# Transforming by mirrored pairs of places: the spectral mixing kernel with 64-point stages in quarters of the array

## The chip, the cores and the metric

The kernel runs on one core of one Trainium2 chip. The metric is the device time of one launch in microseconds; for the kernel before, the median of three runs is given. Where a profile is read, it is one profiled execution, which has a time and a span of its own.

## What is computed

The input x has 8 batches of 3008 places and 256 channels. Each batch is filtered in the frequency domain along the places, and every row then goes through a two-layer network with a "snake" activation:

```python
X = np.fft.rfft(x, axis=1)
y = np.fft.irfft(X * (filt_r + 1j * filt_i), n=3008, axis=1)     # (8, 3008, 256)
h = y.reshape(24064, 256) @ w_in                                # (24064, 2048)
s = np.sin(alpha * h)
out = (h + s * s / (alpha + 1e-9)) @ w_out                      # (24064, 256), float32
```

## The kernel before

3008 is 47 x 64, and a transform runs as a 47-point stage and a 64-point stage, in fp16 with fp32 sums. A place is `R*m + r` with m from 0 to 46 and r from 0 to 63. Only 24 of the 47 frequencies s of the first stage are kept, since x is real.

For a batch b after the first the steps are:

- `load_x`: the batch goes to SBUF through the POOL queue, cast from fp32 to fp16, with two parts of its rows on partitions 0 to 46 and 64 to 110.
- `f1`: the 47-point stage, four calls of eight matmuls. Each uses 47 rows and 48 columns of one quarter (64 x 64) of the array, streams 512 columns, and has the same table `wq`. Four PSUM banks are emptied by ACT and DVE into `asb`, and `asb` is written to a DRAM scratch `scr1`.
- `shuffle1`: reads the scratch back as `bint`, with the places r and the two complex parts on the 128 partitions and the frequency s on the free axis. It is three DMAs on SP's queue.
- `f2x`: the 64-point stage, 24 matmuls of 128 x 128 by 256 columns. Each s has a table of its own in `wb`, since the twiddle factors are inside.
- `swap` and `product`: the product with the filter. Real and imaginary parts lie 64 partitions apart, so from the third batch on two DMAs from SBUF to SBUF swap the halves; the first and second batch have other ways.
- `f2g`, `shuffle2`, `f3`: the way back, again with 24 matmuls with tables of their own (`wg`), a DRAM scratch `scr2`, and a 47-point stage by `we`, which gives the rows of the network transposed, in `yt`.

The network works in 47 chunks g of 512 rows. A chunk has 16 blocks j of the hidden layer: `mlp_in` (two matmuls of 512 columns into a bank `ph`, and on ACT the sine into `vt`), `square` on DVE, and one chunk later the second layer, `mlp_out` for chunks 0 to 3 and `fast_out` (seven products in place of eight, with sums on DVE in `fast_sum`) for the later ones but the last. `out_last` does the last chunk alone, and `store_out` writes 128 rows at a time with DMAs on SP's queue, in the last chunk on SP's and ACT's.

The order is written by hand. A chunk is eight slots of two half slots; a half slot is one `mlp_in` and a share of the second layer. `plan` maps a half slot to the transform steps that are put in it, and `at(slot, f, ...)` fills it. While the network of one batch runs, the transform of the next is done between its matmuls. Every engine runs its instructions in program order.

The first batch can't hide behind a network. It stays on the chip: `f1_chip`, `turn1`, `f2x`, `product`, `g_chip`, `turn2` in an order of its own, with `keep_busy` matmuls of zeros between them. `fold_filter` copies the filter to the upper 64 partitions, and `negate_filter` changes its sign later.

PSUM has three banks `psf` (tag f) for the transform, three banks `psh` (tag ph) for `mlp_in`, and two `pso` for the second layer. `xt` and `bint` share one buffer (tag xb), and so do `asb` and `gsb` (tag ag).

`store_out` cuts a piece of n rows, where n is over 16, to a multiple of 16 and does the rest in a DMA of its own:

```python
n = min(GT - col, 128 - p)
n = n // 16 * 16 or n
```

Of the kernel before, what the change touches and what calls it, by code (L numbers as in the profile page):

```python
# [9 lines left out]
FP16 = mybir.dt.float16  # L10
FP32 = mybir.dt.float32
# [5 lines left out]
GT = 2 * MT  # L17


def dft_tables():  # L20

    m = np.arange(MT)
    k1 = np.arange(NK)
    ang = 2 * np.pi * np.outer(m, k1) / MT
    fa = np.concatenate([np.cos(ang), -np.sin(ang)], 1) / np.sqrt(MT)
    wa = np.zeros((MT, 2, 2, 2 * NK))
    wa[:, 0, 0] = fa  # L30
    wa[:, 1, 1] = fa
    wa = wa.reshape(2 * MT, 4 * NK)
    wa2 = wa.reshape(2 * MT, 4, NK).transpose(0, 2, 1).reshape(2 * MT, 4 * NK)

    we = wa.T.copy()
    we2 = wa2.T.copy()
    wq = np.zeros((2, 64, 64))
    wq[:, 0:MT, 0:2 * NK] = fa
    wq = wq.reshape(128, 64)
    r = np.arange(R)  # L40
    wb = np.zeros((2, R, NK, 128))
    wg = np.zeros((128, NK, 2, R))
    q = 1 / np.sqrt(R)
    d, j, di, ji = slice(0, 32), slice(32, 64), slice(64, 96), slice(96, 128)
    for s in range(NK):
        kd = s + MT * np.arange(32)
        kj = MT * np.arange(1, 33) - s
        td = 2 * np.pi * (np.outer(r, kd) % S) / S
        tj = 2 * np.pi * (np.outer(r, kj) % S) / S
        cd, sd, cj, sj = np.cos(td) * q, np.sin(td) * q, np.cos(tj) * q, np.sin(tj) * q  # L50
        wb[0, :, s, d], wb[1, :, s, d], wb[0, :, s, di], wb[1, :, s, di] = (
            cd, sd, -sd, cd)
        wb[0, :, s, j], wb[1, :, s, j], wb[0, :, s, ji], wb[1, :, s, ji] = (
            cj, -sj, -sj, -cj)
        wd = np.where((kd == 0) | (kd == S // 2), 1.0, 2.0)[:, None]
        wj = np.where(kj == S // 2, 1.0, 0.0 if s == 0 else 2.0)[:, None]
        wg[d, s, 0], wg[di, s, 0], wg[d, s, 1], wg[di, s, 1] = (
            wd * v.T for v in (cd, -sd, sd, cd))
        wg[j, s, 0], wg[ji, s, 0], wg[j, s, 1], wg[ji, s, 1] = (
            wj * v.T for v in (cj, -sj, -sj, -cj))  # L60

    wb = wb.reshape(2, 2, RP, NK * 128).transpose(2, 1, 0, 3).reshape(128, NK * 128)
    wg = wg.reshape(128, NK, 2, 2, RP).transpose(0, 1, 4, 3, 2).reshape(128, NK * 128)
    wgs = np.concatenate([wg[64:], -wg[:64]], 0)
    return [a.astype(np.float16) for a in (wq, wb, wg, we, wa2, we2, wgs)]

@with_exitstack
def kernel(
# [17 lines left out]
    wq_np, wb_np, wg_np, we_np, wa2_np, we2_np, wgs_np = dft_tables()  # L86
    wq_d = nc.inline_tensor(wq_np, name="wq_tbl")
    wb_d = nc.inline_tensor(wb_np, name="wb_tbl")
    wg_d = nc.inline_tensor(wg_np, name="wg_tbl")
    we_d = nc.inline_tensor(we_np, name="we_tbl")  # L90
    wa2_d = nc.inline_tensor(wa2_np, name="wa2_tbl")
    we2_d = nc.inline_tensor(we2_np, name="we2_tbl")
    wgs_d = nc.inline_tensor(wgs_np, name="wgs_tbl")
# [18 lines left out]
    wq = cpool.tile([128, 64], FP16, name="wq")  # L112
    we = cpool.tile([4 * NK, GT], FP16, name="we")
    wa2 = cpool.tile([GT, 4 * NK], FP16, name="wa2")
    we2 = cpool.tile([4 * NK, GT], FP16, name="we2")
    wb = cpool.tile([128, NK * 128], FP16, name="wb")
    wg = cpool.tile([128, NK * 128], FP16, name="wg")
    fri = cpool.tile([128, 2, NK, C], FP16, name="fri")
    w_in16 = tpool.tile([128, 2, DFF], FP16, name="w_in16", tag="tb")
    w_ina = cpool.tile([128, 2, DFF], FP16, name="w_ina")  # L120
# [6 lines left out]
    xt, asb, scr1, bint, xs, z, t2, gsb, scr2, gin, yt, vt, po, ot, x_dma, w_in_dma, filter_dma, swap_dma = (  # L127
# [7 lines left out]
    def load_x(b, parts=2):  # L135

        xt[b] = (xbpool if b else vpool).tile([128 if b else GT, RP, C], FP16, name="xt", tag="xb" if b else "vt")
        n = RP // parts
        for h in range(parts):
            for p0, p1, row, step in (((0, 32, 0, R), (32, MT, 32 * R, R), (64, 96, RP, R), (96, 64 + MT, 32 * R + RP, R))  # L140
                                      if b else ((0, 80, 0, RP), (80, GT, 80 * RP, RP))):
                x_dma[b, h] = nc.gpsimd.dma_start(  # L142
                    out=xt[b][p0:p1, n * h:n * h + n, :],
                    in_=dram(x, (b * S + row + n * h) * C, [[step * C, p1 - p0], [1, n * C]]))
                if b > 2 and h == p0 == 0:
                    gate(x_dma[b, 0], swap_dma[b - 1, 5])

    def f1(b, u):

        if u == 0:  # L150
            asb[b] = agpool.tile([128, 2, RP // 2, C], FP16, name="asb", tag="ag")
            scr1[b] = dpool.tile([RP, 4 * NK, C], FP16, name="scr1", tag="scr1")
        v, w2 = divmod(u, 2)
        ps = [(psh if i == 3 else psf).tile([128, 2, C], FP32, name="psa", tag="ph" if i == 3 else "f")
              for i in range(4)]
        for i in range(2):
            w = 2 * w2 + i
            for h in range(2):
                r0 = 16 * v + 8 * h + 2 * w
                for a in range(2):  # L160
                    nc.tensor.matmul(out=ps[2 * i + a][64 * h:64 * h + 64], lhsT=wq[64 * a:64 * a + MT],  # L161
                                     rhs=xt[b][64 * a:64 * a + MT, r0:r0 + 2, :], start=True, stop=True)
            for a in range(2):
                k = 8 * v + 2 * w
                (nc.vector.tensor_copy if a == 1 and not i else nc.scalar.copy)(  # L165
                    out=asb[b][0:112, a, k:k + 2, :], in_=ps[2 * i + a][0:112])
        if w2:
            for h in range(2):
                r0 = 16 * v + 8 * h
                for a in range(2):  # L170
                    nc.sync.dma_start(
                        out=scr1[b][r0:r0 + 8, 2 * NK * a:2 * NK * a + 2 * NK].rearrange("r q c -> q r c"),
                        in_=asb[b][64 * h:64 * h + 2 * NK, a, 8 * v:8 * v + 8, :])

    def f1_chip(k):

        for half in range(2):
            ps = (psf if half else psh).tile([128, 4, 4 * NK], FP32, name="psa0", tag="f" if half else "ph")
            for i in range(4):
                nc.tensor.matmul(out=ps[:, i, :], lhsT=xt[0][:, 4 * k + i, 128 * half:128 * half + 128],  # L180
                                 rhs=wa2, start=True, stop=True)
            (nc.vector.tensor_copy if half else nc.scalar.copy)(
                out=a_c[:, half, :, 16 * k:16 * k + 16].rearrange("p s (r a) -> p s r a", a=4),
                in_=ps.rearrange("p r (s a) -> p s r a", a=4))

    def turn1(t):

        ps = psh.tile([128, 2, C], FP32, name="pst1", tag="ph")
        for i in range(2):
            for half in range(2):  # L190
                nc.tensor.matmul(out=ps[:, i, 128 * half:128 * half + 128],
                                 lhsT=a_c[:, half, 2 * t + i, :], rhs=ident, start=True, stop=True)
        (nc.vector.tensor_copy if t in (0, 5) else nc.scalar.copy)(
            out=bint[0][:, 2 * t:2 * t + 2, :], in_=ps)

    def g_chip(k, half, i0=0, n=4, act=True):

        ps = (psh if half else pso).tile([128, 4, 128], FP32, name="psg0", tag="ph" if half else f"po{k % 2}")
        for i in range(i0, i0 + n):
            for v, w in ((z, wg), (t2, wgs)):  # L200
                nc.tensor.matmul(out=ps[:, i - i0, :], lhsT=v[k][:, i, 128 * half:128 * half + 128],
                                 rhs=w[:, 128 * (4 * k + i):128 * (4 * k + i) + 128],
                                 start=(v is z), stop=(v is t2))
        (nc.scalar.copy if act and (k, half) != (4, 1) else nc.vector.tensor_copy)(
            out=b_c[:, half, :, 4 * k + i0:4 * k + i0 + n, :],
            in_=ps[:, 0:n].rearrange("p s (r a) -> p r s a", a=4))

    def turn2(j):

        ps = (psf if j < 4 else pso).tile([4 * NK, 2, C], FP32, name="pst2", tag="f" if j < 4 else f"po{j % 2}")  # L210
        rows = b_c.rearrange("p h r s a -> p h r (s a)")
        for i in range(2):
            for half in range(2):
                nc.tensor.matmul(out=ps[:, i, 128 * half:128 * half + 128],
                                 lhsT=rows[:, half, 2 * j + i], rhs=ident, start=True, stop=True)
        (nc.scalar.copy if j in (0, 2, 3, 7, 8) else nc.vector.tensor_copy)(
            out=gin[0][:, 2 * j:2 * j + 2, :], in_=ps)

    def shuffle1(b):
        bint[b] = xbpool.tile([128, NK, C], FP16, name="bint", tag="xb")  # L220
        rows = scr1[b].rearrange("r (a s) c -> (r a) s c", s=NK)
        for sg in range(3):
            nc.sync.dma_start(out=bint[b][:, 8 * sg:8 * sg + 8, :],
                              in_=rows[:, 8 * sg:8 * sg + 8, :])

    def f2x(b, t):
        ps = psf.tile([128, 2, C], FP32, name="psx", tag="f")
# [493 lines left out]
```

## Time and profile before

| what | value |
|---|---|
| median of three runs | 790.77 us (790.77 to 792.18) |
| the profiled execution | 789.34 us |
| its span, first to last instruction | 787.5 us |
| granted TensorE clock, mean | 0.999 |
| PE busy | 773.4 us, 8623 matmuls |
| DVE busy | 696.1 us |
| ACT busy | 659.0 us |
| DMA | 74463 packets, 101.08 MB |
| end of the first stage (first `mlp_in`) | 35.2 us |
| last matmul | starts at 783.4 us |

Busy times are sums over the whole span; a matmul's duration includes its way through the array, so that durations overlap and the start-to-start time says what a matmul costs. A line number such as L161 is the line of the kernel before. "a<-b" reads "a is written from b". In a group, the numbers behind the first bar are busy time and mean duration, and behind the second the engine's idle time ahead of the group with what ended it.

### The profile page before, as it was taken

The page shows a single profiled execution, that of the slowest core. Times are in us where ns is not written, and L with a number is a line of the kernel's source. Part 1 is how long each engine was busy: PE and PEld are TensorE (multiplying, and loading weights), DVE is VectorE, ACT ScalarE, POOL GpSimd, SP SyncE. Part 2 cuts the span into 40 slices and gives each one's busy share as a digit, 9 for nine tenths or more (in the row PEclk, how much of TensorE's full clock was granted, in tenths as well). Part 3 has the DMA queues.
Part 4 walks back from the last instruction along what each step waited for, and adds up shares of the span by engine and source line. Part 5 has one row for each costly group of instructions (what it writes and reads, how often), then busy time and mean ns, then how long its engine had stood idle before and what let it go on. Part 6 is the DMA issues. An engine that isn't in the chain of part 4 may idle for free.

```text
span 787.5 us, 20811 instructions
## 1 busy us (share of the span) xinstructions
PE 773.4 (98%) x8623; PEld 561.5 (71%) x8623; DVE 696.1 (88%) x992; ACT 659.0 (84%) x1316; POOL 53.2 (7%) x104
## 2 busy tenths in 40 slices
PE   6899999999999999999999999999999999999998
PEld 4657666777677776777767777777767777777776
DVE  4896987899889998899898998899988999888894
ACT  4897988898888989798888888889888898777773
POOL 6600020002000020000200010000200000000000
PEclk9999999999999999999999999999999999999999
DMA  9977377434862367633865249623675234321122
GB/s 200 196 117 253 109 187 164 136 105 117 195 177 82 114 147 158 179 87 90 179 142 161 82 102 198 185 80 94 149 196 165 81 108 107 71 55 28 29 55 54
DMA packets 74463, 101.08 MB, mean 128 GB/s; under 512 B 7897, under 2 KB 54761, under 8 KB 72857
## 3 DMA queue, kind: packets, MB, share of 16 engines
q1 hardware_dynamic: 65136, 78.39, 36.8%
q0 software_dynamic: 8704, 21.24, 14.0%
q8 instruction: 67, 1.10, 0.6%
q14 instruction: 28, 0.22, 0.1%
q10 hardware_dynamic: 528, 0.13, 0.1%
HBM read 59.62 MB, written 46.66 MB: 135 GB/s over the span
## 4 chain that ended last, share of the span: by engine, by line
PE 91%; DMA 5%; DVE 2%; ACT 1%; issue 1%; POOL 0%; ACTq 0%; DVEq 0%; POOLq 0%
PE ph L312 40%; PE pf L399 37%; PE po L331 4%; PE psy L296 3%; PE psg L268 2%; PE psx L229 2%; PE psa L161 2%; DMA xt<-in_x_dram 1%; DMA bint<-scr 1%; DMA wgs<-wgs_tbl 1%; PE pe L438 1%; DMA w_in<-in_moe_w_in_dram 1%; ACT vt L314 1%; DMA wb<-wb_tbl 1%; PE psm L503 0%
## 5 line engine op out<-in xcount | busy, mean ns | idle before, releaser
L314 ACT ACTIVATE vt<-ph 128x512 f16<-128x512 f32 x688 | 408.2, 606 | 85.9 <-PE ph L312 76.2
L312 PE MATMUL ph<-yt,w_ina 128*128 128x512 f16 x1376 | 409.9, 380 | 0.0
L399 PEld LDWEIGHTS <-vt 128*128 128x128 f16 x3360 | 231.4, 98 | 104.7 <-DVE ot L413 0.9
L319 DVE TENSOR_TENSOR vt<-vt 128x2048 f16<-128x2048 f16 x188 | 229.3, 1220 | 19.1 <-ACT vt L314 17.8
L399 PE MATMUL pf<-w_out,vt 128*128 128x128 f16 x2016 | 174.5, 220 | 0.2 <-DVE ot L413 0.2
L399 PEld LDWEIGHTS <-s 128*128 128x128 f16 x1344 | 92.6, 98 | 39.8
L413 DVE TENSOR_TENSOR ot<-pf,ot 128x512 f32<-128x512 f32 (+1 forms) x168 | 93.4, 556 | 29.0 <-PE pf L399 26.1
L399 PE MATMUL pf<-tb,s 128*128 128x128 f16 x1344 | 116.2, 220 | 0.0
L399 PE MATMUL pf<-tb,vt 128*128 128x128 f16 x1344 | 116.2, 220 | 0.0
L312 PEld LDWEIGHTS <-w_ina 128*128 128x128 f16 x1376 | 107.0, 98 | 12.1 <-issue 9.6
L142 POOL DMA_DIRECT2D xt<-in_x_dram x72 | 36.6, 516 | 459.2 <-PE ph L312 354.0
L233 ACT CAST xs<-psx 128x512 f16<-128x512 f32 x94 | 56.1, 602 | 3.5 <-PE psx L229 1.1
L270 ACT CAST gsb<-psg 128x512 f16<-128x512 f32 x84 | 48.9, 590 | 4.3 <-PE psg L268 1.2
L358 DVE TENSOR_TENSOR vt<-vt 128x2048 f16<-128x2048 f16 x42 | 51.2, 1219 | 0.0
L358 DVE TENSOR_TENSOR s<-vt 128x2048 f16<-128x2048 f16 x42 | 51.2, 1219 | 0.0
L358 DVE TENSOR_TENSOR s<-s,vt 128x2048 f16<-128x2048 f16 x42 | 51.2, 1219 | 0.0
L358 DVE TENSOR_TENSOR vt<-vt,s 128x2048 f16<-128x2048 f16 x42 | 51.1, 1216 | 0.0
L314 ACT ACTIVATE vt<-ph,alpha_t 128x512 f16<-128x512 f32 x64 | 42.8, 711 | 6.0 <-PE ph L312 5.7
L165 ACT CAST asb<-psa 112x512 f16<-112x512 f32 x84 | 43.7, 596 | 4.6 <-PE psa L161 4.2
L298 ACT CAST yt<-psy 128x376 f16<-128x376 f32 (+45 forms) x126 | 46.4, 369 | 1.1 <-PE psy L296 0.2
L296 PE MATMUL psy<-we,gin 96*128 96x94 f16 x512 | 42.3, 205 | 0.3 <-ACT asb L165 0.3
L331 PE MATMUL po<-w_out,vt 128*128 128x256 f16 x256 | 37.1, 273 | 0.9 <-DVE ot L449 0.9
(96 smaller groups left out, 775.1 us busy)
## 6 DMA issues: line engine op xcount, KB each, us to landing
scr<-asb SPq DMA_DIRECT2D x56, 192.0 KB
bint<-scr SPq DMA_DIRECT2D x21, 512.0 KB
scr<-gsb SPq DMA_DIRECT2D x21, 512.0 KB
out_dram<-ot SPq DMA_DIRECT2D x31, 320.0 KB
t<-xs SPq DMA_DIRECT2D x72, 128.0 KB
xt<-in_x_dram POOLq DMA_DIRECT2D x24, 256.0 KB, 6.6
gin<-scr SPq DMA_DIRECT2D x7, 768.0 KB
out_dram<-ot SPq DMA_DIRECT2D x16, 256.0 KB
```

Source lines behind the costliest of these rows:

```text
L165: (nc.vector.tensor_copy if a == 1 and not i else nc.scalar.copy)(out=asb[b][0:112, a, k:k + 2, :], in_=ps[2 * i + a][0:112])
L233: (nc.vector.tensor_copy if b == 0 and t in (4, 5) else nc.scalar.copy)(out=xs[b, t // 2][:, t % 2 * 2:t % 2 * 2 + 2, :], in_=ps)
L270: nc.scalar.copy(out=gsb[b][:, 2 * t:2 * t + 2, :], in_=ps)
L296: nc.tensor.matmul(out=ps[:, t, :], lhsT=gin[b][:, 4 * a + t, 128 * cb:128 * cb + 128], rhs=we if b else we2, start=True, stop=True)
L298: (nc.vector.tensor_copy if G < 2 and cb == 0 else nc.scalar.copy)(out=yt[g][:, cb, :, lo:lo + n], in_=ps[:, :, 0:n])
L312: nc.tensor.matmul(out=ph, lhsT=(w_in16 if g < 4 else w_ina)[:, cb, 128 * jb:128 * jb + 128], rhs=yt[g][:, cb], start=(cb == 0), stop=(cb ...
L314: nc.scalar.activation(out=vt[g][:, jb, :], in_=ph, func=AFT.Sin, scale=alpha_t[:, jb:jb + 1] if g < 4 else 1.0)
L319: nc.vector.tensor_tensor(out=v4, in0=v4, in1=v4, op=ALU.mult)
L331: nc.tensor.matmul(out=po[g, h][:, i, :], lhsT=vt[g][:, k, ts] if k < 16 else yt[g][:, k - 16, t], rhs=w_out2[:, row(k), :], start=(n == 0 ...
L358: nc.vector.tensor_tensor(out=o, in0=a, in1=b, op=op)
L399: nc.tensor.matmul(out=ps[:, part, i], lhsT=a, rhs=b, start=first, stop=last)
L413: add = lambda out, in0, in1: nc.vector.tensor_tensor(out=out, in0=in0, in1=in1, op=ALU.add)
```

## The change

A place is now written as one of a mirrored pair: `R*m + (j + 0.5)` or `R*m - (j + 0.5)` about a shifted origin, for j from 0 to 31, with the two places of a pair in the 94 rows of one matmul.

- The 47-point stage has a table for each j (`wq1`, 94 x 96 for each of 32), which holds the twiddle factors. `f1` has 16 calls a batch of two full matmuls of 256 columns. `f1_chip` uses `wq`, two quarters of which are loaded and two made on DVE with a sign.
- The 64-point stage has one 64 x 64 table for all s. `f2x` does two groups k at a time in eight quarter matmuls of 512 columns, into four banks; `f2x_out` empties the second pair half a slot later. `f2g` and `f2g_out` do the same on the way back, with the first group split for the frequency 0.
- Real and imaginary part of a value lie on one partition, so `swap` and `fold_filter` fall away. The product takes the filter by a broadcast and reads the other part by a reversed axis.
- `f3` uses a table for each place (`we`, 94 columns for each of 32).
- The mirrored half of x is read row by row, backwards. `shuffle1` has twelve DMAs in place of three, `shuffle2` six in place of three. `store_out` has pieces of at most 47 rows, and in the last chunk leaves their size whole.
- `w_ina` shares a buffer with `b_c` and the late `we`; every slot of the transform's plan is set anew, with three rows of slots for the second, third and later batches.

The core of the diff:

```diff
-        ps = [(psh if i == 3 else psf).tile([128, 2, C], FP32, name="psa", tag="ph" if i == 3 else "f")
-              for i in range(4)]
...
+        ps = psf.tile([4 * NK, 2, C], FP32, name="psa", tag="f")
         for i in range(2):
+            nc.tensor.matmul(out=ps[:, i, :], lhsT=wq1[:, 2 * u + i, :], rhs=xt[b][:, 2 * u + i, :],
+                             start=True, stop=True)
+        (nc.vector.tensor_copy if u % 4 == 1 else nc.scalar.copy)(out=asb[b][:, 2 * u:2 * u + 2, :], in_=ps)
+        if u % 4 == 3:
+            nc.sync.dma_start(out=scr1[b][r0:r0 + 8].rearrange("r q c -> q r c"), in_=asb[b][:, r0:r0 + 8, :])
...
+        for sg in range(3):                                            # shuffle1
+            for a in range(4):
+                nc.sync.dma_start(out=bint[b][32 * a:32 * a + 32, 8 * sg:8 * sg + 8, :],
+                                  in_=rows[a, :, 8 * sg:8 * sg + 8, :])
...
+    def quarters(n, name):
+        return [(psf if i else psh).tile([128, 2, C], FP32, name=name, tag="f" if i else "ph")
+                for i in range(n)]
+    def f2x(b, ks, dve=()):
+        ps = quarters(2 * len(ks), "psx")
+        for n, k in enumerate(ks):
+            for o in range(2):
+                for part in range(2):
+                    p = slice(64 * part, 64 * part + 64)
+                    nc.tensor.matmul(out=ps[2 * n + part][64 * o:64 * o + 64], lhsT=wb[p],
+                                     rhs=bint[b][p, 4 * k + o:4 * k + o + 3:2, :], start=True, stop=True)
+            bank[b, k] = ps[2 * n:2 * n + 2]
+        f2x_out(b, ks[0], dve)
...
+            nc.vector.tensor_tensor(out=z[k], in0=xs[b, k], op=ALU.mult,          # product
+                                    in1=fr[:, ks].unsqueeze(1).broadcast_to([128, 2, 2, C]))
+                nc.vector.tensor_tensor(out=t2[k], in0=xs[b, k][:, ::-1], in1=fi[:, :, ks], op=ALU.mult)
...
+            for p0, p1 in ((0, 32), (32, MT)) if b else ((0, MT),):               # load_x
+                for a in range(2):
+                    row = R * p0 + (RP - 1 - n * h if a else RP + n * h)
+                    x_dma[b, h] = nc.gpsimd.dma_start(
+                        out=xt[b][MT * a + p0:MT * a + p1, n * h:n * h + n, :],
+                        in_=dram(x, (b * S + row) * C, [[R * C, p1 - p0], [-C if a else C, n], [1, C]]))
...
-            n = min(GT - col, 128 - p)                                            # store_out
-            n = n // 16 * 16 or n
+            half, m = divmod(col, MT)
+            n = min(MT - m, 128 - p)
+            n = n if g == NCH - 1 else n // 16 * 16 or n
...
+    LATER = (-17.5, 0.75, -4.0, (-1.5, 6.5, 15.5), (0.5, 0.5, 4.5, 7.0, 7.0, 8.0), 10.5, 28.0, 18.0)
+        for u in range(16):
+            at(p + u0 + gap * u, f1, b, u)
+        at(p + sh, shuffle1, b)
...
-        nc.sync.dma_start(out=wa2, in_=wa2_d.ap())
+        nc.sync.dma_start(out=wq[:, 0:4:2], in_=wq_d.ap())
...
+        gate(nc.sync.dma_start(out=we0[:, 8:], in_=we0_d.ap()[:, 8 * GT:]), w_in_dma[1, 1])
+        nc.sync.dma_start(out=wq1, in_=wq1_d.ap())
```

`wq` has 94 rows of 2 x 1536 bytes and `wq1` 94 rows of 6144 bytes. In `LATER` the entries are the slots of the first f1 and the step between f1 calls, of `shuffle1`, of the three f2x, of the six products, of `f2g` behind its f2x, of `shuffle2` and of `load_x`, counted from p = 48 (b - 1).

## The prediction

> **What bounds the kernel now.** I read the page first: its busy shares, then its chain.
>
> ```profile
> PE 773.4 (98%) x8623; PEld 561.5 (71%) x8623; DVE 696.1 (88%) x992; ACT 659.0 (84%) x1316; POOL 53.2 (7%) x104
> PE 91%; DMA 5%; DVE 2%; ACT 1%; issue 1%; POOL 0%; ACTq 0%; DVEq 0%; POOLq 0%
> ```
>
> Averages over stages with different limits, so I asked next for the windows (length, then busy time and count of PE, PEld, DVE, ACT, POOL, clock, DMA share, GB/s):
>
> ```profile
> 0.00:35.00 35.00, 27.17 (x299) 18.64 (x300) 22.02 (x41) 22.45 (x45) 21.18 (x43) 1.00 1.02 206
> 35.00:60.00 25.00, 24.16 (x211) 14.23 (x209) 21.38 (x40) 24.21 (x48) 6.00 (x11) 1.00 0.72 115
> 129.00:222.00 93.00, 93.00 (x1078) 68.01 (x1077) 87.13 (x123) 82.02 (x168) 4.04 (x8) 1.00 0.53 132
> ```
>
> Three regimes. To 35 us the sixteen DMA engines are full (share 1.02). To 60 ACT is full. From 60 us PE never stops; a batch is 93 us, DVE at 94%, ACT at 88%. So a PE microsecond removed there is a microsecond, and one lost before 60 us is not won back later.
>
> The transform's PE work in the groups view (busy, mean ns of one | idle):
>
> ```profile
> L161 PE MATMUL psa<-xt,wq 47*64 47x512 f16 x224 | 17.9, 389 | 0.0
> L229 PE MATMUL psx<-bint,wb 128*128 128x256 f16 x192 | 36.2, 273 | 1.0 <-DMA bint<-scr 0.7 <-DVE bint L193 0.3
> L268 PE MATMUL psg<-z,wg 128*128 128x256 f16 x168 | 31.1, 273 | 0.0
> ```
>
> Durations overlap there, so I use start-to-start times from the timeline: 216 ns for 512 columns, 109 for 256, 56 for 128, 41 for 94.
>
> ```profile
> 205.62 0.39 PE L399 MATMUL pf<-tb,vt 128*128 128x128 f16 x4
> 205.94 0.63 PE L161 MATMUL psa<-xt,wq 47*64 47x512 f16 x8
> 206.50 0.60 PE L312 MATMUL ph<-yt,w_ina 128*128 128x512 f16 x2
> ```
>
> Eight quarter matmuls of f1 start in two bunches of four, 0.24 us apart: four share the array. The group holds PE 0.56 us, and the first starts 149 ns after its predecessor instead of 56: 0.65 us in all, where perfect sharing would be 0.43.
>
> **Steady stage.** Per batch from the second on, f1 goes from 4 quarter groups (2.60) to 32 full matmuls of 256 columns (32 x 0.109 = 3.49). f2x goes from 24 x 0.109 = 2.62 to 3 quarter groups, 1.95; f2g from 2.62 to 1.95 plus two split matmuls (0 to 0.2, take 0.1). Sum 7.84 to 7.49: 0.35 saved, times 7 is **-2.4 us**. The Trainium skill (TensorEngine Tiling (Array Packing), Performance Considerations) says that tiling speeds up TensorE and not PSUM evacuation. By it the saving would be 0. The trace leans against it while PE is the full engine: the old f1 groups also fill four banks, and every start of L312 behind L399 from 130 to 770 us comes after 55 to 57 ns.
>
> Evictions keep count and size (16, 12, 12 a batch), products too (3 x 6; the second batch drops six half ones). A broadcast operand has no 16-bit row here; the strided 2048-element sums take 1219 ns like flat squares, so 686 ns stays; at the fp32 rate of L413 it would double for 12 products a batch, 8 us of DVE against 6 idle. I take 0. Four-bank groups put 4 x 0.6 us on ACT over two half slots; old f1 put 3 and one on DVE and PE did not wait. Take 0, bound 12 (0.3 x 42 groups).
>
> The swaps go (72 transfers of 128 KB, on no chain): 0.
>
> **The shuffle's distance.** The old last f1 group starts at 404.37; its writes leave at 405.92, the reads at 413.31, f2x runs at 417.13:
>
> ```profile
> 405.92 3.23 SPq L171 DMA_DIRECT2D scr<-asb  x4
> 413.31 2.16 SPq L223 DMA_DIRECT2D bint<-scr  x3
> ```
>
> 12.8 us for 13 half slots, just covered (0.7 us of waits on bint in all). The new plan leaves 10 half slots, about 9.4 us (0.87 each and four f3). The last write is half as large (768 packets fewer, -2.4 us), goes after one eviction (-0.4), but the first third needs four reads (+1.2): 11.2 us needed. PE is in order, so up to 1.8 us is lost in each of five batches and 3 in the second; SP holds nothing urgent behind that wait. Bounds 0 to 12; take **+6**.
>
> **Which DMA engines a transfer uses** decides the rest. The DMA view of the first 3 us, and of the tail:
>
> ```profile
> q1 hardware_dynamic: 240, 0.05, 7.9%
> ident<-id_tbl SPq DMA_DIRECT2D x1, 32.0 KB
> wa<-wa_tbl SPq DMA_DIRECT2D x1, 17.6 KB
> ...
> q10 hardware_dynamic: 96, 0.07, 3.0%
> out_dram<-ot ACTq DMA_DIRECT2D x2, 2.0 KB
> out_dram<-ot ACTq DMA_DIRECT2D x2, 14.0 KB
> ```
>
> q1 moved wa (94 rows) and ident (128): 222 data packets of 240, so 18 closing ones, 16 + 2: the 94-row table ran on two engines. q10's pieces of 2 and 14 rows have one closer a row (48 + 48). Over the run q1 has 5570 four-byte packets in the packet records. The largest number up to 16 that divides a transfer's rows, summed over all SP transfers, is exactly 5570; min(rows, 16) would be 5584. So on SP and ACT 34 rows use 2 engines, 94 use 2, and 47 (a prime) use one. The change puts such transfers in three places where the old kernel split them or had them tiny. The Trainium skill (DMA: Bandwidth & Descriptors, Why a DMA increments its semaphore by 16 and not by 1) states the same divisor rule, with 127 partitions on one engine; the trace agrees at 94 rows.
>
> **Tail.** `store_out` leaves the last chunk's pieces whole: 34, 47 and 47 rows, three calls. Engine 0 carries 17 + 47 + 47 = 111 packets each time. A packet of 2048 bytes takes 82 ns, of 1024 bytes 45 (packet records): 9.1 + 5.0 + 5.0 = 19.1 us from 781.1, where the first call's packets start, to 800.2; the old last packet ends at 785.97. **+14.2 us**, covered by nothing.
>
> **Start.** First consumer behind the DMA queue is w_out: its halves are issued at 39.30 and land at 47.8 and 50.4, and the second chunk opens on them:
>
> ```profile
> 48.91 0.86 DVE L484 TENSOR_SCALAR w_out<-w_out,recip 128x256 f16<-128x256 f16 x4
> 50.42 0.71 PE L331 MATMUL po<-w_out,vt 128*128 128x256 f16 x5
> ```
>
> Slack 1.1 us. Work of one engine up to the first half of w_out, before (packet ns: 322 for 4 KB out of 8 KB fp32, 60 for 512 bytes out of 1 KB, 158 for a plain 4 KB, 173 for w_in): x 7.6, filters 9.6, tables 5.9, w_in 5.5, x of the second batch 7.6, w_out 3.8: 40.0, and 40.7 on the two engines that ran wa. After, on an even engine: x 9.4 (its mirrored half goes row by row: 188 x 322 + 1504 x 60 ns over 16), filters 11.5 (all rows of 1 KB), tables 2.2, w_in 5.5, x again 9.4, w_out 3.8: 41.8. On the two engines that carry wq and wq1 there is more: wq 94 packets of 1536 bytes at 64 ns (between 46 and 81) 5.9; wq1 47 of 6 KB at 240 (on the line through 81 and 159) 11.3: 59.0. Each load of x, filters and weights needs all engines, so all wait for these two: w_out 18.3 us later, less 1.1, **+17.2 us**. Earlier waits lie inside it: f1_chip starts when wq lands, about 15 us instead of 7.5 (94 packets taking turns with x); the last filter lands 5 later; f1 of the second batch waits for wq1. The dropped fold_filter copies (4.9 us of DVE) hide behind these landings: 0. Bounds: 0.7 if the two tables spread, 33 in the worst case of the second rival.
>
> **Sum** on the profiled run's own time, 789.34 us (span 787.5): -2.4 + 6 + 14.2 + 17.2 = +35, 824.3. The median of the runs shown is 1.4 above that run: **825**.
>
> **Rivals.**
> *Everything spreads* (the other side): 34-, 47- and 94-row transfers use all engines. Then w_out comes 1.8 us later, 0.7 beyond its slack, the tail is 0.3 shorter with three transfers for four, and if the writes of f1 land in time the PE saving decides: 790.8 - 2.4 + 0.7 - 0.3 = 789. It turns to slower once the shuffle waits exceed 2.0 us in all, 0.4 in each of five batches. For it: a start with less to move (2.4 MB of tables ahead of w_out before, 1.6 after). Against: 240 packets, and 5570. 0.10.
> *47 rows on one engine in the software queue too.* The first batch's x goes through POOL in 47-row transfers. For the spread over 16: the 14- and 15-row POOL transfers show 40 packets more than 16 each, one filler for each engine without a row. If not, a mirrored part takes 376 x 60 ns = 22.6 us on one engine, x lands near 29 (last issue 5.0, 1.4 to the first packet) where the sum above has 19 (2.6, 9.4 and 5.9, and the receipt), and all loads behind it move by 10 us more, or by 16 where such a part meets wq's engine: 835 to 841. 0.08. The same section of the Trainium skill has its divisor rule for both queues, except for some direct copies of the software one; no row here has a prime above 16 on that queue.
> *Only one of the two places bites*: the tail alone (wq served ahead of x, wq1 behind w_out), 803 to 809 with shuffle waits of 0 to 6, or the start alone, 811. 0.17.
> *Forecast as summed*, 815 to 833: 0.62. Left, 0.03: no change within error by cancelling terms.
>
> **Numbers.** Predicted 825. From 803 to 840 takes the forecast, the one-place cases and most of the bounds; below lies the first rival, above the second. What a measurement can tell from no change is about 0.2%, 1.6 us (the three runs differ by 1.4). Faster 0.09, same 0.03, slower 0.88.
>
> **What would show it.** Right: in the tail, packets on for 19 us after the first store of the last chunk with a DMA share near 1/16; PE idle from about 7 to 15 us before L180's successor, released by wq's DMA; PE waiting for wq1 in the first chunk and DVE for w_out before the second; L229's successor waiting on bint by 1 to 2 us a batch; quarter groups of 0.65 us in f2x and f2g, f1 pairs of 0.22. Wrong: a tail of 6 us after the last matmul, f1_chip at 8 us, mlp_in at 35: then the transfers spread. Quarter groups over 0.65, or L312 late behind them, would mean PSUM and not DMA.

## The result and the profile after

The changed kernel takes **850.9 us** (median of four runs, 850.1 to 851.1) against 791.1 for the kernel before in the same comparison: 1.075 times as long, 95% interval 1.073 to 1.077. The prediction was 825, range 803 to 840. The direction and two of the four terms held (PE and the tail); the start cost far more than its term, and the shuffle nothing.

Where it went is read from the trace as the start of each chunk's first `mlp_in` matmul (us):

| | before | after | difference |
|---|---|---|---|
| chunk 0 starts | 35.2 | 76.0 | +40.8 |
| chunk 6 starts | 139.7 | 188.8 | +49.1 |
| chunk 46 starts | 761.7 | 808.5 | +46.8 |
| last matmul | 783.4 | 830.2 | +46.8 |
| end of the span | 787.5 | 849.3 | +61.8 |

So the start costs 49.1, the steady stage gives back 2.3, and the tail costs 15.0. The page, first its busy times, then the software queue (POOL's) and the chain:

```profile
PE 778.7 (92%) x8698; PEld 559.6 (66%) x8698; DVE 687.7 (81%) x983; ACT 653.6 (77%) x1311; POOL 64.4 (8%) x101
...
q0 software_dynamic: 43344, 19.23, 16.3%
...
PE 86%; DMA 6%; issue 3%; POOL 2%; DVE 1%; ACT 0%; DVEq 0%; POOLq 0%
```

PE is as busy as before, in a longer span; "issue" and POOL have grown in the chain (1% and 0% before), and the software queue has 43344 packets where it had 8704, for fewer bytes. The windows, with the start and the tail on their own:

```profile
0.00:55.00 55.00, 12.35 (x145) 7.11 (x146) 5.37 (x14) 5.00 (x10) 18.66 (x22) 1.00 0.54 48
55.00:100.00 45.00, 36.25 (x343) 24.50 (x341) 28.80 (x46) 32.22 (x63) 16.75 (x29) 0.89 0.83 128
178.00:271.00 93.00, 92.91 (x1077) 66.89 (x1075) 86.81 (x124) 79.86 (x163) 4.56 (x8) 1.00 0.50 119
815.00:849.00 34.00, 15.48 (x160) 12.48 (x158) 8.20 (x12) 6.49 (x12) 0.00 (x0) 0.77 0.11 31
```

For 55 us little computes and the DMA engines move 48 GB/s (the 1.00 of that row for the clock is no measurement: the clock records of this profile begin at 58.4 us); the kernel before moved 206 in its first 35. In the steady stage PE is full. The tail's DMA share is 0.11, about one or two engines of 16.

What PE waited for up to 130 us (total, times, longest), and POOL up to 60:

```profile
PE psa L159 <- DMA xt<-in_x_dram: 20.1, 3, 14.8
PE psa L159 <- issue: 10.4, 1, 10.4
...
PE psa L146 <- DMA wq<-wq_tbl: 6.4, 1, 6.4
```

```profile
POOL xt L135 <- issue: 19.5, 2, 18.4
```

The start waits for x, line 135, and x waits for POOL, which stands for 18.4 us inside the issue of x's loads. POOL's timeline (start, length) and the DMA view of the first 54 us show what it is doing:

```profile
1.25 7.33 POOL L135 DMA_DIRECT2D xt<-in_x_dram  x5 [0.80 <-POOLq L707]
26.96 3.33 POOL L135 DMA_DIRECT2D xt<-in_x_dram  x2 [18.38 <-issue]
31.43 2.81 POOL L135 DMA_DIRECT2D xt<-in_x_dram  x1 [1.15 <-issue]
```

```profile
q0 software_dynamic: 25328, 2.06, 50.6%
xt<-in_x_dram POOLq DMA_DIRECT2D x8, 188.0 KB, 22.5
```

Of x's four parts, the forward half (47 rows of 4 KB) lands 5.7 us after its issue in the first part; the other three land 19 to 24 us after theirs, each within 1 us of the mirrored half issued ahead of it. The mirrored halves (47 rows of eight times 512 bytes) were issued at 1.89, 5.25, 26.96 and 31.43 and landed at 26.62, 31.10, 48.16 and 53.55. POOL spends 2.8 us on issuing each, where other loads take 0.5. The packet records have 22,796 packets of four bytes on this queue from 2 to 54 us: 15 for each of the 4 x 376 row packets make 22,560. So one engine carries the rows, and the other 15 get a filler for each row. The third mirrored load leaves 0.34 us after the first has landed, the fourth 0.33 after the second: two at a time fit into the queue.

In the steady stage the groups that answer to those of before:

```profile
L146 PE MATMUL psa<-xt,wq 94*96 94x256 f16 x224 | 44.0, 278 | 6.4 <-DMA wq<-wq_tbl 6.4
L220 PE MATMUL psx<-bint,wb 64*64 64x512 f16 x192 | 16.1, 392 | 0.1
L261 PE MATMUL psg<-z,wg 64*64 64x512 f16 x154 | 13.5, 387 | 0.1
```

Behind the last f1 (at 367.0 in one batch), the write and the twelve reads on SP's queue, and the first f2x:

```profile
367.93 0.32 SPq L151 DMA_DIRECT2D scr<-asb  x1
371.14 6.43 SPq L206 DMA_DIRECT2D bint<-scr  x12
376.30 0.63 PE L220 MATMUL psx<-bint,wb 64*64 64x512 f16 x8
```

The mean busy share of the DMA engines in the last 20 us, in 40 slices (tenths):

```profile
DMA  1010000000000001100000110000000000000000
```

That is the tail on one engine, as drawn in the prediction: the last matmul starts at 830.2, packets run on to 848.0. Those of the last chunk take 20.2 us from the first (827.8), where the prediction had 19.1.

### The profile page after: what moved, and what is told of

Same layout as the page of the kernel before. It is cut to its first block, busy times and chain, and to the rows that moved or that the text cites. A ratio compares the mean times of both kernels' runs of the same rounds, so it can differ in the third digit from the quotient of the medians.

```text
span 849.3 us, 21163 instructions
## 1 busy us (share of the span) xinstructions
PE 778.7 (92%) x8698; PEld 559.6 (66%) x8698; DVE 687.7 (81%) x983; ACT 653.6 (77%) x1311; POOL 64.4 (8%) x101
## 3 DMA queue, kind: packets, MB, share of 16 engines
q0 software_dynamic: 43344, 19.23, 16.3%
## 4 chain that ended last, share of the span: by engine, by line
PE 86%; DMA 6%; issue 3%; POOL 2%; DVE 1%; ACT 0%; DVEq 0%; POOLq 0%
PE ph L313 38%; PE pf L400 35%; DMA xt<-in_x_dram 5%; PE po L332 4%; PE psa L146 3%; PE psy L297 3%; POOL xt L135 2%; PE psx L220 1%; PE psg L261 1%; PE pe L439 1%; DMA w_out<-in_moe_w_out_dram 1%; DMA fi<-in_filt_i_dram 1%; PE psm L505 0%; POOL fr L541 0%; POOL fi L541 0%
## 5 line engine op out<-in xcount | busy, mean ns | idle before, releaser
L313 PE MATMUL ph<-yt,late 128*128 128x512 f16 x1376 | 409.6, 379 | 0.0
L400 PEld LDWEIGHTS <-vt 128*128 128x128 f16 x3360 | 231.3, 98 | 104.5 <-DVE ot L414 0.3
L400 PE MATMUL pf<-w_out,vt 128*128 128x128 f16 x2016 | 174.2, 219 | 0.0
L400 PEld LDWEIGHTS <-s 128*128 128x128 f16 x1344 | 92.5, 98 | 39.8
L313 PEld LDWEIGHTS <-late 128*128 128x128 f16 x1376 | 106.4, 98 | 15.6 <-issue 14.0
L400 PE MATMUL pf<-tb,s 128*128 128x128 f16 x1344 | 116.1, 219 | 0.0
L400 PE MATMUL pf<-tb,vt 128*128 128x128 f16 x1344 | 116.1, 219 | 0.0
L135 POOL DMA_DIRECT2D xt<-in_x_dram x72 | 49.7, 701 | 479.9 <-PE psx L220 439.1
L148 ACT CAST asb<-psa 96x512 f16<-96x512 f32 x84 | 49.0, 584 | 10.6 <-PE psa L146 7.1
L229 ACT CAST xs<-psx 128x512 f16<-128x512 f32 x94 | 51.2, 607 | 4.9 <-PE psx L220 4.6
L146 PE MATMUL psa<-xt,wq 94*96 94x256 f16 x224 | 44.0, 278 | 6.4 <-DMA wq<-wq_tbl 6.4
L270 ACT CAST gsb<-psg 128x512 f16<-128x512 f32 x84 | 46.8, 635 | 1.2 <-PE psg L261 1.2
L161 ACT CAST a_c<-psa 128x384 f16<-128x384 f32 x8 | 3.8, 479 | 47.7 <-PE psa L159 47.7
```

What stands on the lines that cost most here:

```text
L135: x_dma[b, h] = nc.gpsimd.dma_start(out=xt[b][MT * a + p0:MT * a + p1, n * h:n * h + n, :], in_=dram(x, (b * S + row) * C, [[R * C, p1 - p ...
L146: nc.tensor.matmul(out=ps[:, i, :], lhsT=wq1[:, 2 * u + i, :], rhs=xt[b][:, 2 * u + i, :], start=True, stop=True)
L148: (nc.vector.tensor_copy if u % 4 == 1 else nc.scalar.copy)(out=asb[b][:, 2 * u:2 * u + 2, :], in_=ps)
L229: (nc.vector.tensor_copy if part in dve else nc.scalar.copy)(out=xs[b, k][:, part], in_=bank[b, k][part])
L270: nc.scalar.copy(out=gsb[b][:, o, 2 * k:2 * k + 2, :], in_=bank[b, k][o])
L313: nc.tensor.matmul(out=ph, lhsT=(w_in16 if g < 4 else late["w_ina"])[:, cb, 128 * jb:128 * jb + 128], rhs=yt[g][:, cb], start=(cb == 0), s ...
```

## The experiments

The theory drawn from this profile (A): the loss is rows on few DMA engines, in three places (x, the tables, the last stores), and nothing else. The rivals are named in each expectation. Starts of chunk 6 show what each run did to the start, and "tail" is last matmul to end.

| run | time | ratio to before (95%) | x(0) landed | chunk 6 | chunk 46 | tail |
|---|---|---|---|---|---|---|
| before | 790 to 791 | | 12.9 | 139.7 | 761.7 | 4.1 |
| after | 850.9 | 1.073 to 1.077 | 53.6 | 188.8 | 808.5 | 19.1 |
| x in 32 + 15 rows | 815.0 | 1.031 to 1.035 | 17.8 | 152.7 | 772.0 | 19.1 |
| last stores cut | 837.4 | 1.059 to 1.062 | | 188.0 | 807.5 | 6.7 |
| tables in 80 + 14 | 838.8 | 1.061 to 1.065 | 49.3 | 178.8 | 798.1 | 19.5 |
| all three | 791.4 | 1.001 to 1.004 | 14.0 | 143.0 | 762.3 | 7.2 |

**x alone.** The pieces of the later batches, for the first batch too:

```diff
-            for p0, p1 in ((0, 32), (32, MT)) if b else ((0, MT),):
+            for p0, p1 in ((0, 32), (32, MT)):
```

> Undoes one part: both halves of the first batch's x are loaded as 32 and 15 rows again, as the later batches' are. Theory A (the mirrored 47-row load runs on one DMA engine, with a four-byte filler on each of the other 15 for every row, and POOL can hold only two such loads): the 22560 or so fillers go, x(0) lands by 16 to 20 us instead of 53.5, the third load's 18 us wait on POOL is gone, f1_chip ends near 22 instead of 55, and the time falls by about 30 to 34 us, to 817 to 821; what is left over before is the tail's 15 and about 17 of wq and wq1, as the prediction had it. Theory B (reading mirrored rows of 512 bytes is slow whatever the row count, or the 94-row tables bound the start): x or wq still lands after 40 us and the time stays above 840.

Measured: 815.0, 36 us less and 2 below the interval. x lands at 17.8, POOL's longest wait within it is 2.3 us, the fillers are gone (20944 packets). Theory A holds, B falls. What DVE waits for first is now the table:

```profile
DVE wq L637 <- DMA wq<-wq_tbl: 12.1, 1, 12.1
```

This run is also the prediction's own scene, with x spread as it had assumed. The first half of w_out, for which the prediction had 18.3 us, lands at 63.0, 15.3 us later than the 47.8 of before (the second at 67.6, 17.2 later). Chunk 6 starts 13.0 us later than before; the term was 17.2.

**The last stores alone.**

```diff
-            n = n if g == NCH - 1 else n // 16 * 16 or n
+            n = n // 16 * 16 or n
```

> Undoes one part: the last chunk's stores go in pieces of 16, 32 or 48 rows and a rest again. Theory A (34, 47 and 47 rows run on 2, 1 and 1 DMA engines): from the last matmul to the end 4 to 5 us instead of 19.1, the time 835 to 837. Theory B (the end is late for another reason, such as the queue still being behind from the start): the tail stays over 12 us and the time over 843.

Measured: 837.4, a tail of 6.7. A holds, with 2 us more left over than expected.

**The tables alone.**

```diff
-        nc.sync.dma_start(out=wq[:, 0:4:2], in_=wq_d.ap())
+        for p0, p1 in ((0, 80), (80, GT)):
+            nc.sync.dma_start(out=wq[p0:p1, 0:4:2], in_=wq_d.ap()[p0:p1])
```

and the same for `wq1`.

> Undoes one part: wq and wq1 are loaded as 80 and 14 rows instead of 94. Theory A (the start is set by x): x(0) still lands at 53 us; only the 6 to 7 us that the second batch's f1 waits for wq1 and the share of it in w_out can go: 842 to 849. Theory C (the prediction's own term: the two engines that carry the 94-row tables hold back all loads behind them): the start shortens by about 17 us, to 832 to 836.

Measured: 838.8, between the two cases and in neither: the start shortens by 10. So C's mechanism is real but smaller, and A as stated missed a part: x itself lands 4.3 us earlier. In the packet records a mirrored load's rows come every 114 ns up to 11.5 us in the changed kernel, as long as 1536-byte packets of `wq` run on (its 94 rows on two engines; the last starts at 11.47), and every 41 ns from 12.6 us on; here the last such packet starts at 4.5 us and the rows, from the first at 5.5, come every 41 ns but for a few gaps. A likely reading is an engine shared by the two; the records don't number the engines.

**All three.**

> All three parts at once: x(0) in 32 and 15 rows, the tables in 80 and 14, the last stores in multiples of 16. If row counts on few DMA engines are the whole of the loss (A), the start and the tail are as before within 2 us and the steady stage's 2 to 3 us of PE decide: 787 to 793, first matmul at 8 to 12 us, last matmul 781 to 785. If something else of the change costs in the start (more row-wise loads, waits for the shuffle), it shows here alone: over 796.

Measured: 791.4, 1.8 us above the 789.7 beside it (0.1 to 0.4%). Of the 61.8 us of span that the change had cost, 3.6 are left: +3.3 at chunk 6, -2.7 from there to chunk 46, +3.0 in the tail. So rows on few engines are the whole of the loss but these 3.6. What the 3.3 and 3.0 are, the waits of PE up to 130 us and of SP at the end tell:

```profile
PE po L332 <- DVE w_inT L499: 2.3, 1, 2.3
```

```profile
SPq L461 <- DMA out_dram<-ot: 5.4, 6, 3.1
```

The first half of w_out lands at 51.7 against 47.8 (the second at 56.3 against 50.4), behind the second batch's x, of whose 16 loads half now read 120 or 256 rows of 512 bytes; PE's wait ends on DVE's work behind that landing, at 52.8. And SP holds a late store back for 3.1 us until an earlier one has landed.

**Only the mirrored half split.**

```diff
-            for p0, p1 in ((0, 32), (32, MT)) if b else ((0, MT),):
-                for a in range(2):
+            for a, p0, p1 in (((0, 0, 32), (1, 0, 32), (0, 32, MT), (1, 32, MT)) if b
+                              else ((0, 0, MT), (1, 0, 32), (1, 32, MT))):
```

> Of the first batch's x only the mirrored half, read row by row (512 bytes each), is loaded as 32 and 15 rows; the forward half stays one transfer of 47 rows of 4 KB. If the price hangs on the mirrored half alone (theory A; the forward halves landed 4 to 6 us after their issue already), this equals the run with both halves split, 815: 812 to 818, and the software queue's packets fall from 43344 to about 20800. If a prime number of rows costs by itself, also in the 4 KB form (theory D), x(0) still lands late by ten us or more: over 825.

Measured: 819.5 (1.035 to 1.039), outside the expected interval. The software queue has 20880 packets, as A has it, and x lands at 18.1, as with both halves split: a prime number of 4 KB rows costs no landing time here, so D falls. (The ground that the expectation gives, forward halves that had all landed in 4 to 6 us, held for the first alone.) The other 4.5 us arise later. The first half of w_out lands at 65.8 instead of 63.0, PE waits 4.4 for it in place of 0.9, and the granted clock falls to 0.5 while it waits (64.7 to 71.5 us), so that PE runs 4.5 us at half speed. That is 3.5 us more of waiting and 2.3 of slow clock; from chunk 1 to chunk 6 this run takes 5.7 us longer than the one with both halves split. The windows from 60 to 75 us, first with both halves split, then with one:

```profile
60.00:75.00 15.00, 14.13 (x115) 10.52 (x114) 11.43 (x28) 13.30 (x24) 0.00 (x0) 1.00 0.83 169
```

```profile
60.00:75.00 15.00, 10.60 (x71) 7.30 (x70) 7.97 (x20) 8.60 (x16) 0.00 (x0) 0.77 0.81 154
```

Why w_out landed later there is not known.

**Another composite.** The mirrored half as 34 and 13 rows, to test the law and not only its cure:

```diff
...
+                              else ((0, 0, MT), (1, 0, 34), (1, 34, MT))):
```

> Tests the law, not just the cure: the mirrored half of the first batch's x as 34 and 13 rows. If the number of engines is the largest divisor of the rows up to 16 (A), 34 rows run on 2 engines with 14 x 136 fillers and 13 rows on 13 with 3 x 8, so 4 x 1928 = 7712 fillers in place of 22560: the software queue has about 28500 packets in place of 43344, a 34-row part takes 136 x 41 ns = 5.6 us in its engines instead of 15.6, x(0) lands by 16 to 26 us, and the time is 816 to 826. If any count that isn't a multiple of 16 runs on one engine (E), the time stays near 840 or above and the packets near 33000 or more; if only a prime is bad (F), the packets are near 20800 and the time is 815.

```profile
q0 software_dynamic: 28560, 19.17, 15.5%
```

Measured: 28560 packets, against 20880 with 32 + 15. The difference, 7680, is 4 x (14 x 136 + 3 x 8) less the 32 fillers of the 15-row parts, to the packet. So the divisor rule decides the number of engines for these loads; E and F fall. The time is 827.0, one above the interval; x lands at 28.1 where 16 to 26 was expected, with a wait of 8.2 us on POOL (the tenth load leaves 0.28 us after the second, a part of 34 rows, has landed at 16.7; why that part took 14.8 us is not shown).

**Eight parts of 47 rows.**

```diff
-        load_x(0, 4)
+        load_x(0, 8)
```

> The changed kernel with one edit: the first batch's x is loaded in eight parts in place of four, still 47 rows each (mirrored transfers of 188 row packets in place of 376). The work of one engine for the mirrored rows is the same (1504 packets, 22560 fillers). Theory G (POOL's queue holds a fixed amount of entries, some 12000 with the fillers, so two of the old transfers and four of the new ones, each on an engine of its own): the third and fourth leave without a wait, four engines share the rows and x(0) lands at 25 to 35 us instead of 53.5: 822 to 836. Theory H (two such transfers at a time, whatever their size): the third still waits for the first to land, four pairs of 10 to 13 us each follow one another, x(0) lands at 45 to 55: 842 to 855.

Measured: 836.3. POOL's timeline:

```profile
1.24 10.81 POOL L135 DMA_DIRECT2D xt<-in_x_dram  x9 [0.80 <-POOLq L707]
18.75 7.79 POOL L135 DMA_DIRECT2D xt<-in_x_dram  x6 [6.70 <-DMA xt<-in_x_dram]
```

Four mirrored loads leave without a wait inside an issue; the first stop is 6.7 us for a completion. H falls: it is not two transfers, whatever their size. For G speaks that halving the size let at least twice as many leave. Where the room ends isn't seen here, for this stop is of another kind: a load waits for the one eight before it to land. The tenth leaves 0.28 us after the second has landed; with x in 32 + 15 rows, almost without fillers, the ninth leaves 0.28 after the first and the tenth 0.29 after the second. So a fixed room of some 12,000 entries is a reading, not a measured limit. G's price was too low: x lands at 39.9, not by 35, and the time is 0.3 above its interval.

**The tail's rule on the kernel before.**

```diff
-            n = n // 16 * 16 or n
+            n = n if g == NCH - 1 else n // 16 * 16 or n
```

> The kernel before, with one edit: the last chunk's stores are not cut to multiples of 16 (pieces of 34 and 94 rows). By the divisor rule (A) both run on two engines, 64 packets of a call on the fullest engine: 64 x 82 + 2 x 64 x 45 ns = 11 us from 781.1, which ends 6 us later than before: 794 to 798 against 790, a tail of about 10 us. If such stores spread, or the tail of the changed kernel came from something else, no change within 2 us.

Measured: 797.7, 1.008 to 1.012 times the kernel before: 7.7 by the medians, 7.1 by the spans. The tail is 11.5 us. From the last matmul on, one queue carries most of it (278 of 359 packets):

```profile
DMA  2000110111111111111111111111111110000000
q10 hardware_dynamic: 278, 0.36, 9.0%
```

A holds, without any other part of the change.

**f3's output.** PE's matmuls of f3 start 44.7 ns apart, 42.1 before. Their output goes to PSUM in two pieces now.

```diff
-            nc.tensor.matmul(out=halves[:, first:first + step + 1:step], ...
+            nc.tensor.matmul(out=ps[:, t, :], ...
```

> The changed kernel with the output of f3's matmuls written as one piece of 94 columns in place of two pieces of 47 that lie 47 or more columns apart in PSUM. It leaves out the interleaving of the two halves (the places come out in another order). Theory P (the two-piece output costs the 2.7 ns by which f3's matmuls are slower than before, 44.7 against 42.0 ns start to start): 42 ns again, 1.4 us less over the run. Theory Q (it is the table, which now changes with each matmul): 44.7 ns stay.

Measured: 850.3 in one run, and 44.7 ns as ever between chunks 12 and 42. P falls. That the table changes with each matmul is what is left of what was named; it wasn't tried by itself.

**A version that gains.** All three parts split, and the two leftovers taken out (the new argument of `load_x` names the parts to load):

```diff
-        load_x(1, 4)
+        load_x(1, 4, (0, 1))
         load_w_out(0)
         load_w_out(1)
+        load_x(1, 4, (2, 3))
...
-                    store_out(g - 1, 0, 4, (nc.sync,))
+                    store_out(g - 1, 0, 4, (nc.sync, nc.gpsimd) if g == NCH - 1 else (nc.sync,))
```

In the first form the last chunk's stores went to SP, ACT and POOL:

> The version with all three parts split, and two more edits: w_out is loaded between the halves of the second batch's x instead of behind them, and the stores of the last two chunks are dealt to SP, ACT and POOL in turn (in the version with all parts split, SP's last stores waited 3.1 us for the completion of an earlier one). If the 2 us that it loses in the first six chunks come from w_out landing 6 us later than before, and the 3 us at the end from that wait, both go and the 3 us of the steady stage are left: 785 to 788. If x's later half then makes f1 of the second batch wait, or POOL's stores land later, 789 to 793.

Measured: 787.9, 0.9957 to 0.9982 of before, with a tail of 5.9. In the second form they go to SP and ACT, as before:

> As the version that gained (all three parts split, w_out ahead of the second half of the second batch's x, the next-to-last chunk's stores dealt to SP and POOL), but the last chunk's stores go to SP and ACT alone again, as in the kernel before. If POOL's last stores stretch the end (5.9 us from the last matmul to the end there, 4.1 before, 7.2 without POOL), the tail falls to 4.5 to 5.5 us and the time to 786 to 788; if POOL is needed to keep SP and ACT from waiting for completions, the tail is 6 to 7 us and the time 788 to 790.

Measured: **786.8, 0.9948 of the kernel before (0.9932 to 0.9963)**, with a tail of 4.1, that of the kernel before. Chunk 6 starts at 139.4 (0.3 earlier than before), chunk 46 at 759.2 (2.5 earlier). Its windows of the first two stages:

```profile
0.00:35.00 35.00, 26.29 (x343) 17.53 (x344) 19.55 (x37) 20.30 (x39) 25.42 (x49) 1.00 1.03 161
35.00:60.00 25.00, 24.74 (x217) 17.54 (x215) 21.24 (x42) 24.43 (x50) 5.53 (x10) 1.00 1.01 186
```

The DMA engines are full again in both, as they were before only in the first, and PE is busy for 24.7 of 25 us. The kernel before wasn't run with these two edits of order, so how much of them it would share is open; its tail is the same 4.1.

## Why the prediction was right or wrong, step by step

**The start is the step that failed** (+17.2 in the sum, +49.1 measured at chunk 6). In its sum x was "188 x 322 + 1504 x 60 ns over 16". Its mirrored half doesn't run on 16 engines but on one, two such loads at a time, and x landed at 53.6 where the sum had 19. The ground for the spread was the 40 packets of the 14- and 15-row POOL transfers; but 14 divides by 14 and 15 by 15, so the divisor rule gives the same 14 and 15 engines with the same fillers. The row was no evidence between the two cases, and the rival deserved far more than 0.08. The Trainium skill (DMA: Bandwidth & Descriptors, Why a DMA increments its semaphore by 16 and not by 1) has the rule for both queues, with an exception for some direct copies of the software one; the trace agrees with it for the rows of 512 bytes (22,560 fillers, and 7712 for 34 + 13), and the 4 KB forward half is of the exception's kind: beside the 22,560 there are 236 four-byte packets, where one engine for its rows too would have made 2820 more.

**The rival named the cause and still mis-sized it.** It had x landing near 29 and 835 to 841 us; x landed at 53.6. Its 22.6 us for a mirrored part were near the measured time from issue to landing (21 to 26), but by luck: rows come every 41 ns and not 60, 15.4 us for 376 of them, and the first load's first row comes 6.9 us after its issue. Missing was that the parts follow one another in pairs, since the third can't be issued until the first has landed: two rounds and not one, 24.6 us more of x for 10 to 16 us more of time than it gave.

**The term of wq, wq1 and w_out was right in kind, too large in effect**: 18.3 predicted for the first half of w_out and 15.3 measured with x spread; but of the time, taking the tables away gives 10.0 (alone) or 9.7 (on top of x) at chunk 6. The remaining 3.3 is w_out behind the many small reads of x, of which the prediction had 0.7; with the order of the two changed it is gone. Together: x 36.1, tables 9.7, rest 3.3, sum 49.1.

**The tail**: 14.2 predicted, 15.0 measured, 12.4 of it undone by cutting the pieces (19.1 to 6.7). The count of packets on engine 0 carried over from 2 and 14 rows to 34 and 47, and to the kernel before (6 expected, 7 measured).

**PE in the steady stage**: -2.4 predicted for the run, -2.3 from chunk 6 to 46. The terms that it had are right, one is missing, and the agreement of the totals is in part luck. Start-to-start sums between chunks 12 and 42, from a matmul's start to that of the next:

| | matmuls before / after | before us, ns each | after us, ns each |
|---|---|---|---|
| f1 | 128 / 128 | 8.93, 69.8 | 14.19, 110.8 |
| f2x | 118 / 112 | 12.89, 109.2 | 7.82, 69.8 |
| f2g | 120 / 130 | 13.11, 109.2 | 8.41, 64.7 |
| f3 | 328 / 328 | 13.81, 42.1 | 14.67, 44.7 |

The 69.8 and 64.7 leave out what comes ahead of a quarter group. Its first matmul starts 149 ns after its predecessor instead of 56, in f1 before as in f2x and f2g after, and this falls to the predecessor's sum (below, the second matmul of L400 starts 56 ns after the first):

```profile
376.10 0.28 PE L400 MATMUL pf<-w_out,vt 128*128 128x128 f16 x2
376.30 0.63 PE L220 MATMUL psx<-bint,wb 64*64 64x512 f16 x8
376.86 0.61 PE L313 MATMUL ph<-yt,late 128*128 128x512 f16 x2
```

With these 93 ns a group costs 8 x 69.8 + 93 = 651 ns, the 0.65 of the prediction. So f1 lost 0.94 a batch (0.89 predicted), f2x gained 0.67 (0.67) and f2g 0.66 (0.57), and f3, which had no term, lost 0.17: -0.2 a batch and not -0.35. From chunk 6 to 46 lie the f1 of five batches (+4.7) and the f2x and f2g of six (-4.5 and -3.6, with the 0.7 us of waits on `bint` that are gone); f3 takes +1.4 and the network's own matmuls -0.3: -2.3, which is near -2.4 in part because of where this stretch begins and ends. The four-bank groups cost nothing at PE, and the changed kernel has no PE wait at all from 130 to 815 us. The rule that spoke against the saving, the Trainium skill's on PSUM evacuation (TensorEngine Tiling (Array Packing), Performance Considerations), took nothing from it here, by the same rows.

**The shuffle's distance**: +6 predicted, 0 measured. The one remaining write is read 3.2 us after its issue and the first third of `bint` is there by 376.3, 9.3 us behind the last f1, inside the 9.4 that the plan leaves. 11.2 had been added up from a transfer of another size; this row was the nearest, and too far: from the write's issue to the first read went from 7.4 us to 3.2, where the sum had taken off 2.4.

**"Everything spreads"**, 789 for 0.10, is near what the version shows whose three parts are split so that they spread: 791.4.

## What to carry to other kernels

Before a transfer's shape is changed, write down its row count and the largest divisor of it up to 16, for each queue: the tables, the loads and the last stores all paid for 47, 94 and 34, and one loop that loads 47 rows as 32 and 15 gives back 36 us. (On the software queue the form counts too: 47 rows of 4 KB spread.) When a row of the trace is taken as evidence between two cases, work out what each case would show in it; a row that both explain decides nothing. And price a serial load by how many fit into the queue at once, not by one alone.

## What the runs showed of the hardware that was not expected

- On the software queue a 47-row load in 512-byte pieces puts all rows on one engine and 15 four-byte packets per row on the others (22,560), costs POOL 2.8 us to issue instead of 0.5, and blocks POOL inside an issue for 18.4 us when a third one comes. The first 47-row load of 4 KB rows beside it landed in 5.7 us, and splitting such loads moved x's landing by only 0.3 us.
- One mirrored load took a 512-byte row every 41 ns, faster than the 60 ns that each packet lasts. Two in flight took 48 rows a us together, 24 each, as on an engine of its own for each.
- In the run with only the mirrored half split, PE waited 4.4 us for w_out. The clock was granted at 0.5 from 64.7 to 71.5 us (0.77 over the window), and matmuls of 256 columns started 0.21 us apart instead of 0.11 for the 4.5 us after the wait: it cost 2.3 us more than its length.
- Six stores of 2 to 32 rows a call in the last chunk, in place of four, came with waits of SP of 5.4 us in all for earlier stores to land; POOL taking a share of the chunk ahead brought the tail back from 7.2 to 4.1.
